# Where the output norms of a kernel's tail put their rows: a ring of five buffers, or eleven tiles that are no longer used

## The chip, the cores and the metric

The kernel runs on one core of a Trainium2 chip. The metric is the device time of one execution in microseconds, as the median of several runs. Engines are named as in the profile: PE is TensorE's matmul row, PEld its weight loads, DVE is VectorE, ACT is ScalarE, POOL is GpSimd and SP is the engine that issues most of the DMAs.

## What is computed

The reference is one conformer block on x of shape 2 x 4000 x 144 in bf16, with four heads of 36:

```python
h = _layernorm(x);  x = x + 0.5 * (_silu(h @ w_ff1a) @ w_ff1b)
h = _layernorm(x);  q, k, v = heads(h @ w_qkv)
p = _softmax(q @ k.T * Dh ** -0.5);  x = x + merge(p @ v) @ w_o
h = _layernorm(x);  a, b = split(h @ w_pw1);  h = a * _sigmoid(b)
c = sum(shift(h, i - 2) * dw[i] for i in range(5))
x = x + _silu(c) @ w_pw2
h = _layernorm(x);  x = x + 0.5 * (_silu(h @ w_ff2a) @ w_ff2b)
return _layernorm(x)
```

This change is about the last line: the layernorm that makes the output, and its way out to memory.

## The kernel before

The 8000 tokens are cut into 16 chunks of 500 (NCH = 16), each held as four blocks of 125 rows in the tile X. Attention over all keys takes most of the time: for each chunk of queries, scores go to PSUM, their exponentials are written by ACT or DVE to one of eleven tiles of PT (128 x 1000 bf16, 2000 bytes a partition), and PE multiplies them with the values. The other stages of the chunks (first feed-forward, projections, gated unit and convolution, second feed-forward, norms) are threaded between the attention's pieces, and what is left of them after the last attention product is the tail.

The program is first recorded: each call of `op` notes an instruction, what it reads and writes by key, and from the history of these keys the earlier instructions that it must wait for. Then `settle` (line 2140) and `arrange` (465) put the instructions of each engine into an order that is written out in a table (ORDER). `finish` (535) turns the dependencies into semaphore waits and drops those that another wait of the same engine already covers, and `replay` (579) emits them. So each engine works through a fixed queue, and an instruction that waits holds up all behind it on its engine. Almost every instruction has line 589 in the profile, because `replay` issues them there; they are told apart by their tiles.

A layernorm is `ln` (1236). It takes one of five buffers u of XN (NXN = 5, line 795; 2048 bytes a partition each), makes statistics on DVE (tile ST, key MV), the scale on POOL or DVE with POOL's power (tile RS, keys VE and RS), and then one instruction for each block of 125 rows on DVE, POOL or ACT that writes the normed rows to XN[u] (key XN). Two kinds of user come next:

- Norms ahead of a matmul (`ln_tr`, 1308): the rows are transposed, by PE through PSUM for small parts of the last chunks and by a DMA on SP for whole chunks.
- Output norms (`store`, 1872, with `store=True`): the rows lie packed in XN[u] (the view XNC, 1020) and `put` (1866) issues one DMA that writes them to the output. In the tail this DMA may be issued by SP or by ACT.

The buffer's key orders its users: the next norm with the same u writes after the last transposes or the last store have finished reading. A store has finished when its DMA has landed, so a norm can wait for a store. The statistics' keys order the same way, but only norms read them.

In the tail (`mode["tail"]`, set at 2450, after the last attention product is recorded) nine output norms are recorded: chunk 9, chunk 10, chunk 14's blocks 2 and 3, its blocks 0 and 1, chunk 13, chunk 11, chunk 12, and chunk 15's two halves. Chunks 14 and 15 go in halves of two blocks. On DVE's queue stand, in this order: chunk 9's output norm, chunk 15's second-half norm ahead of its gated unit, chunk 10's output norm, the output norm of chunk 14's blocks 0 and 1, the norm of chunk 12 ahead of its second feed-forward (four instructions), the norms of chunk 15's second and first half ahead of theirs (two each), and then the output norms of chunks 13, 12 and of chunk 15's first half. Chunk 11's output norm is POOL's; those of chunk 14's and 15's second halves are ACT's.

PSUM has eight banks. The last two (BX = 6 and 7) hold the attention sums; once the attention is over, bank 6 is given to the other stages as well (2452).

Of the kernel before, what the change touches and what calls it, by code (L numbers as in the profile page):

```python
# [12 lines left out]
D = 144  # L13
H = 4
DH = 36
HD = 72
# [5 lines left out]
TB = 125  # L22
NB = 4
CH = 500
# [269 lines left out]
    'ddadppdadppdddddppdpddppdppdddddddddddppadadppdddppadppddddddppdddddppdadappdppddppddddppdppdddppddp'  # L294
    'pdddppddpddppddappdddppdppddddppddpddppddppddppddddddpppdddaapppdddaadppdppppddddapddddaaddddddaaddd'
    'addddpdddpddadddddddpdpddpddapddddddpddaaddddad'
)
ALPHABET = '!#$%&()*+,-./0123456789:;<=>?@ABCDEFGHIJKLMNOPQRSTUVWXYZ[]^_`abcdefghijklmnopqrstuvwxyz{|}~'

# [5 lines left out]
def c_dve(n, rate=1.0):  # L305
    return n / (960 * rate) + 0.07
# [456 lines left out]
def bass_standalone__conformer_family_zipformer__speech_kernel(  # L763
# [24 lines left out]
    R = Rec(nc)  # L788
# [178 lines left out]
    XN = sb("XN", [NXN, NB, 2, 128])  # L967
# [14 lines left out]
    PT = sb("PT", [NPT, 2, CH])  # L982
# [31 lines left out]
    BX = 6  # L1014
    PTU = PT[:, :, :, :].rearrange("p a b n -> p (a b n)").bitcast(U16).rearrange("p (a b n) -> p a b n", a=NPT, b=2)
# [4 lines left out]
    XNC = XN[:, :, :, :, :].rearrange("p u i k n -> p u (i k n)")[:, :, 0:NB * D].rearrange("p u (i d) -> p u i d", i=NB)  # L1020
# [126 lines left out]
        Slots(R, range(n)) for n in (NXN, NXT, NTH - 2, NHT, NSW, NAN, NPT))  # L1147
    thw = Slots(R, [NTH - 2])
    wide = Wide(banks)
    mode = {"front": True, "tail": False}  # L1150
    silus = [6]

    def small(c):
# [81 lines left out]

    def ln(c, bs, e=False, store=False):
        n, b0, rows = len(bs), bs[0], TB + e
        xn = (lambda u, j: XNC[0:rows, u, j, :]) if store else (lambda u, j: XN[0:rows, u, j, :, 0:HD])
        xi = (lambda j: X[0:rows, c * NB + b0 + j, :]) if store else (lambda j: halves(X[0:rows, c * NB + b0 + j, :]))
        xe = ["XE"] * e  # L1240
        u = yield need("dve", xnp)
        for j in range(0, n, 2):
            op("dve", "bn_stats", ST[0:rows, u, j:j + 2, :].rearrange("p i k -> p (i k)"),
               xv(c, range(b0 + j, b0 + j + 2), rows).rearrange("p i d -> p d i"),
               r=[("X", c, b0 + j), ("X", c, b0 + j + 1)] + xe, w=[("MV", u)], cost=0.365)
        calm = small(c)
        if n == NB and not calm and not store and ("XN", u) not in clear:
            clear.add(("XN", u))
            yield need("pool")
            op("pool", "memset", XN[:, u, :, :, :], 0.0, w=[("XN", u)], cost=0.8)  # L1250
        yield need("dve" if calm else "pool", hold=calm)
        a = (RS[0:rows, u, 1, 0:n], ST[0:rows, u, 0:n, 2], 1.0 / D, LN_EPS)
        k = dict(op0=ALU.mult, op1=ALU.add)
        o = op("dve" if calm else "pool", "tensor_scalar", *a, **k, r=[("MV", u)], w=[("VE", u)], cost=0.08 if calm else 0.28)
        if calm:
            R.unit([o], "d", {"p": [("pool", "tensor_scalar", a, k, 0.28, None)]})
            yield need("pool")
        else:
            R.unit([o], "p", {"d": [("dve", "tensor_scalar", a, k, 0.08, None)]})
            R.step += 1  # L1260
        op("pool", "tensor_tensor", RS[0:rows, u, 0, 0:n], RS[0:rows, u, 1, 0:n], NHALF[0:rows, 0:n], op=ALU.pow,
           r=[("VE", u), "NHALF"], w=[("RS", u)], cost=0.7 if calm else POW_COST)
        NM = RS[0:rows, u, 2, 0:n]
        signs = {"p": ("pool", "tensor_scalar", (NM, ST[0:rows, u, 0:n, 1], -1.0, None), dict(op0=ALU.mult), 0.24, None, None, ()),
                 "a": ("dve", "scalar_tensor_tensor", (), dict(
                     out=NM, in0=ST[0:rows, u, 0:n, 1], scalar=-1.0, in1=RS[0:rows, u, 0, 0:n], op0=ALU.mult, op1=ALU.mult),
                     0.08, None, None, ())}
        if not calm:
            code = "p"
            R.step += 1  # L1270
        elif mode["tail"] and R.free["act"] + XSLACK < R.free["dve"]:
            code = "a"
            yield need("dve", hold=True)
        else:
            code = "d"
            yield need("dve")
        pre = []
        if code in signs:
            g = signs.pop(code)
            pre = [op(g[0], g[1], *g[2], **g[3], r=[("MV", u)] + [("RS", u)] * (code == "a"), w=[("NM", u)], cost=g[4])]  # L1280
            if code == "a":
                yield need("act")
            R.step += 1
        alts, ops = {"d": [], "p": [], "a": []}, []
        for j in range(n):
            sc = RS[0:rows, u, 0, j:j + 1]
            k = dict(op1=ALU.mult)
            alts["d"].append(("dve", "tensor_scalar", (xn(u, j), xi(j), ST[0:rows, u, j, 1:2], sc), dict(
                op0=ALU.subtract, op1=ALU.mult), 0.231, None))
            alts["p"].append(("pool", "tensor_scalar", (xn(u, j), xi(j), RS[0:rows, u, 2, j:j + 1], sc), dict(  # L1290
                op0=ALU.add, op1=ALU.mult), XN_COST, XN_LAT))
            alts["a"].append(("act", "activation", (xn(u, j), xi(j), ACT.Identity),
                              dict(bias=RS[0:rows, u, 2, j:j + 1], scale=sc), 0.41, None))
            eng, name, a, k, cost, lat = alts[code][-1]
            ops.append(op(eng, name, *a, **k, r=[("X", c, b0 + j), ("MV", u), ("RS", u)] + [("NM", u)] * bool(pre) + xe,
                          w=[("XN", u)], cost=cost, lat=lat))
        alts.pop(code)
        deps = [(d, True) for key in (("MV", u), ("RS", u)) for d in R.history(key)[0]]
        R.unit(ops, code, alts, {q: [g[:7] + (deps,)] for q, g in signs.items()}, pre=pre)
        R.step += 1  # L1300
        return u

    XSLACK = 3.2
    XN_COST = 0.5
    XN_LAT = 0.4
# [534 lines left out]
    def post2(c):  # L1840
        cc = c % CPB
        last = cc == CPB - 1
        z = yield need("pe", swp, cond=lambda: c in glu_done and (last or c == NCH - 2 or c + 1 in glu_done))
        e = c == NCH - 1
# [21 lines left out]
        def put(dst, src, u):  # L1866
            q = f"o{len(outs)}"
            act = mode["tail"] and R.free["act"] < R.free["sp"]
            op("act" if act else "sp", "dma_start", dst, src, q=q, r=[("XN", u)], cost=0.4 if act else 0.7)
            outs.append(q)  # L1870

        def store(bs):
            n, b0, b1 = len(bs), bs[0], bs[-1] + 1
            u = yield from ln(c, bs, e and 3 in bs, True)
            if c == NCH - 2 and 3 in bs:
                put(out_tok[c][0:TB - 1, b0:b1, :], XNC[0:TB - 1, u, 0:n, :], u)
                if n > 2:
                    put(out_tok[c][TB - 1:TB, b0:2, :], XNC[TB - 1:TB, u, 0:2, :], u)
            else:
                put(out_tok[c][:, b0:b1, :], XNC[0:TB, u, 0:n, :], u)  # L1880
            if e and 3 in bs:
                put(out_tok[c - 1][TB - 1:TB, 2:4, :], XNC[TB:TB + 1, u, 0:2, :], u)
            xnp.give(u)

        def part(bs):
# [10 lines left out]
        ps = parts(c)  # L1896
# [103 lines left out]
            return (PTI[:, z, :, :], PSV[:, lo:hi + 1:hi - lo, 0:CH], EXP_BIAS, 0.0), k  # L2000
        return (PTI[:, z, hh, :], PSV[:, lo, 0:CH], EXP_BIAS, 0.0), k

    def ymw_args(what, z, y):
        zu, yu = (PTU[:, q, :, :].rearrange("p b n -> p (b n)") for q in (z, y))
        zf, yf = (PT[:, q, :, :].rearrange("p b n -> p (b n)") for q in (z, y))
        bits = dict(op0=ALU.bitwise_and, op1=ALU.bitwise_or)
        if what == "y":
            return "tensor_scalar", (yu, zu, 0x7F, 0x3F00), bits
        if what == "m":
            return "tensor_tensor", (yf, zf, yf), dict(op=ALU.mult)  # L2010
        return "tensor_scalar", (zu, zu, 0x7F80, 2), bits
# [122 lines left out]
    for c in range(CPB):  # L2134
        S.add(pre(c), R.ready(("X", c, 0), "dve"), rank=-1 if c == 0 else 1)

    COST = dict(S=0.2105, E=c_act(2 * CH), R=c_act(CH), z=c_dve(CH), x=c_dve(2 * CH), y=c_dve(2 * CH, 4),
                m=c_dve(2 * CH, 2), w=c_dve(2 * CH, 4))

    def settle():  # L2140
        R.choose(UNITS)
# [23 lines left out]
        for k, ops in old.items():  # L2165
            if k[1] == "O":
                sum_deps.setdefault(R.phase[k[0]], {}).update({id(d): (d, raw) for d, raw in outside(ops) if not raw})
        where = 0
        for n in range(NIT):
            ph, c, t = its[n]  # L2170
            rest = t == NF
# [24 lines left out]
            else:  # L2196
# [7 lines left out]
                else:  # L2204
# [5 lines left out]
                deps, last = [(z, True) for z in zs], None  # L2210
                chain = {}
                for i, what in enumerate("ymw"):
                    name, a, k = ymw_args(what, *sl)
                    more = [] if last is None else [(last, True if what == "m" else False)]
                    chain[what] = last = fresh("dve", name, a, k, COST[what], "e", deps + more, (n, what), 2 + i)
                chain["w"].deps.append((chain["y"], False))
                made = {0: (zs, [chain["w"]]), 1: ([chain["y"]], [chain["m"]])}
# [281 lines left out]
```

## Time and profile before

| | |
|---|---|
| median of 3 runs | 868.47 us (868.26 to 868.83) |
| span of the profiled execution, first to last instruction | 866.2 us |
| the execution's time beyond its span, taken as the median less the span | 2.3 us |
| granted TensorE clock over the span | 0.999 |
| last attention product on PE | 820.8 us |
| last instruction of DVE on data | 861.9 us |
| PE busy | 849.7 us (98%) |
| DVE busy | 835.1 us (96%) |
| ACT busy | 834.9 us (96%) |

No other time of the profiled execution is given than its span, so the execution's own time is put at the median. All times in the traces are microseconds from the start of the span. In a row of the timeline stand the start, the length, the engine, the line, the operation, the tile written and those read, the shape, and the number of instructions that were merged into the row; in brackets is the idle time of the engine just before the row and what ended it. A row such as `XN<-X,ST,RS` is a norm, `out_dram<-XN` a store of normed rows, `X<-PS,X` a residual addition out of PSUM, and `PS<-IDENT,XN` a transpose on PE.

### The profile page before, as it was taken

How to read it: one execution, taken by the hardware profiler on the slowest of the kernel's cores; microseconds unless marked ns; L12 is line 12 of the kernel's file. 1: busy time of each engine (PE TensorE's matmuls, PEld its weight loads, DVE VectorE, ACT ScalarE, POOL GpSimd, SP SyncE). 2: the span in 40 equal slices, each digit the busy share in tenths (PEclk: the TensorE clock that was granted, in tenths of full speed). 3: DMA queues.
4: the chain of work that ended last, by engine and by line, in shares of the span. 5: the costliest groups of instructions: out<-in, count | busy, mean ns of one | idle time of the engine just before them, and what ended most of it. 6: DMA issues, size and time to landing. Idle time of an engine off the chain costs nothing.

```text
span 866.2 us, 27018 instructions
## 1 busy us (share of the span) xinstructions
PE 849.7 (98%) x11585; PEld 412.0 (48%) x11585; DVE 835.1 (96%) x1819; ACT 834.9 (96%) x1096; POOL 283.2 (33%) x562
## 2 busy tenths in 40 slices
PE   9999999999999999999999999999999999999996
PEld 8644434444344444444444444445444444445585
DVE  7999999999999999999999999999999999999986
ACT  6999999999999999999999999999999999999975
POOL 7771331041334301441230060320550173300854
PEclk9999999999999999999999999999999999999999
DMA  3331111102113110211210020110130021100121
GB/s 102 83 54 21 33 21 38 21 14 45 34 26 51 17 24 2 51 27 39 33 39 2 2 44 3 21 26 14 26 49 4 12 48 39 26 2 14 41 47 50
DMA packets 86331, 26.92 MB, mean 31 GB/s; under 512 B 81384, under 2 KB 86210, under 8 KB 86210
## 3 DMA queue, kind: packets, MB, share of 16 engines
q1 hardware_dynamic: 84662, 24.34, 15.0%
q8 instruction: 91, 1.49, 0.7%
q10 hardware_dynamic: 1548, 0.84, 0.4%
q14 instruction: 30, 0.25, 0.1%
HBM read 3.31 MB, written 2.30 MB: 6 GB/s over the span
## 4 chain that ended last, share of the span: by engine, by line
ACT 40%; PE 40%; DVE 17%; DMA 1%; issue 0%; POOL 0%; DVEq 0%; ACTq 0%
PE PS L589 40%; ACT PT L589 37%; DVE PT L589 12%; ACT TH L589 3%; DVE ST L589 1%; DVE QT L589 1%; DVE HT L589 1%; DVE U L589 1%; DVE X L589 1%; DMA X<-in_x_dram 0%; DMA out_dram<-XN 0%; DVE XN L589 0%; DVE KT L589 0%; ACT X L589 0%; DVE AN L589 0%
## 5 line engine op out<-in xcount | busy, mean ns | idle before, releaser
L589 ACT ACTIVATE PT<-PS 128x1000 bf16<-128x1000 f32 (+1 forms) x793 | 730.0, 1072 | 4.9 <-PE PS L589 4.1
L589 PE MATMUL PS<-QT,KT 64*64 64x500 bf16 x3968 | 460.2, 383 | 4.2 <-ACT PT L589 1.2
L589 PE MATMUL PS<-PT,VA 64*37 64x500 bf16 x4828 | 449.6, 372 | 1.3 <-DVE QT L589 0.5
L589 DVE TENSOR_SCALAR PT<-PS 128x500 int16<-128x500 f32 x425 | 279.8, 678 | 4.3 <-PE PS L589 2.9
L589 PEld LDWEIGHTS PS<-QT,KT 64*64 64x64 bf16 x3968 | 139.8, 104 | 201.9 <-ACT PT L589 99.9
L589 PEld LDWEIGHTS PS<-PT,VA 64*37 64x37 bf16 x4828 | 163.1, 96 | 105.5 <-issue 16.2
L589 POOL TENSOR_SCALAR RS<-ST 125x4 f32<-125x4 f32 (+1 forms) x132 | 31.0, 237 | 479.9 <-DVE ST L589 476.0
L589 DVE TENSOR_SCALAR PT<-PT 128x1000 uint16<-128x1000 uint16 x430 | 172.6, 419 | 1.8 <-DVE PT L589 0.2
L589 DVE TENSOR_TENSOR PT<-PT 128x1000 bf16<-128x1000 bf16 x215 | 144.9, 678 | 0.8
L589 POOL TENSOR_SCALAR XN<-X,RS 125x144 bf16<-125x144 bf16 x250 | 142.4, 581 | 3.9 <-POOL RS L589 0.5
L589 POOL TENSOR_TENSOR RS<-RS,NHALF 125x4 f32<-125x4 f32 (+2 forms) x93 | 92.0, 993 | 50.7 <-DVE RS L589 48.6
L589 ACT ACTIVATE TH<-PS 128x500 bf16<-128x500 f32 (+3 forms) x175 | 92.8, 560 | 3.5 <-PE PS L589 3.0
L589 DVE SCALAR_TENSOR_TENSOR HT<-TH,PS 128x500 bf16<-128x500 bf16 (+1 forms) x120 | 71.5, 616 | 0.8 <-ACT TH L589 0.5
L589 PE MATMUL PS<-XTB,WA 72*128 72x500 bf16 (+2 forms) x280 | 71.3, 359 | 0.6 <-DVE PT L589 0.2
L589 DVE BATCH_NORM_STATS2 ST<-X 125x6 f32<-125x288 bf16 (+1 forms) x160 | 65.6, 449 | 1.9 <-DMA X<-in_x_dram 1.2
L589 DVE SCALAR_TENSOR_TENSOR X<-PS,X 125x288 bf16<-125x288 f32 x114 | 50.8, 451 | 6.7 <-PE PS L589 5.6
L589 PE MATMUL PS<-WB,HT 128*125 128x144 bf16 (+1 forms) x640 | 52.2, 229 | 0.1
L589 PEld LDWEIGHTS PS<-WB,HT 128*125 128x125 bf16 (+1 forms) x640 | 44.9, 136 | 13.4 <-issue 3.9
L589 PEld LDWEIGHTS PS<-XTB,WA 72*128 72x128 bf16 x280 | 21.5, 97 | 28.9 <-issue 8.3
L589 PE MATMUL PS<-U,DG 128*128 128x375 bf16 (+7 forms) x204 | 28.0, 263 | 0.1
L589 POOL COPY U<-U 128x2 bf16<-128x2 bf16 (+1 forms) x54 | 10.6, 229 | 42.5 <-DVE U L589 32.3
L589 ACT ACTIVATE HT<-PS 128x500 bf16<-128x500 f32 (+3 forms) x43 | 20.6, 537 | 3.4 <-PE PS L589 2.9
(95 smaller groups left out, 522.1 us busy)
## 6 DMA issues: line engine op xcount, KB each, us to landing
X<-in_x_dram SPq DMA_DIRECT2D x16, 140.6 KB
XTQ<-XTB SPq DMA_DIRECT2D x24, 70.3 KB
out_dram<-XN SPq DMA_DIRECT2D x12, 140.6 KB
XTB<-XN SPq DMA_TRANSPOSE x53, 3.6
out_dram<-XN ACTq DMA_DIRECT2D x2, 140.6 KB
XTB<-AN SPq DMA_TRANSPOSE x15, 3.2
WA<-in_w_ff1a_dram ACTq DMA_DIRECT2D x1, 144.0 KB
WB<-in_w_ff1b_dram ACTq DMA_DIRECT2D x1, 144.0 KB, 2.6
```

The lines of the kernel that those rows point to most:

```text
L589: ins = getattr(eng, o.name)(*o.a, **o.k)
```

## The change

An output norm that is recorded in the tail no longer writes to the buffer XN[u]. The first of them writes to tile 0 of PT, the next to tile 1, and so on to tile 8 for the ninth; each tile is used once. Its store reads from there. The norm keeps its number u for its statistics and scales. Three things follow for the waits:

- The norm's instructions drop what they would have waited for because of XN[u].
- In their place they wait for the instructions that last wrote banks 6 and 7 of PSUM as the program is recorded. For bank 7 these are the last attention sums, after which no probability is read. Bank 6 has by then been used by other stages, so the wait is for a matmul of theirs.
- A norm of another kind that gets the same u later drops the tail norms and their stores from what it waits for.

The core of the diff:

```diff
     def ln(c, bs, e=False, store=False):
         n, b0, rows = len(bs), bs[0], TB + e
-        xn = (lambda u, j: XNC[0:rows, u, j, :]) if store else (lambda u, j: XN[0:rows, u, j, :, 0:HD])
+        late = store and mode["tail"]
+        if late:
+            at.append(XPT[:, len(at)])
+            row = at[-1]
+        xn = (lambda u, j: (row[0:rows, j, :] if late else XNC[0:rows, u, j, :])) if store else (lambda u, j: XN[0:rows, u, j, :, 0:HD])
...
         u = yield need("dve", xnp)
+        if late:
+            out_of[u] = row
...
+            h = R.history(("XN", u))
+            before = {id(o) for o in h[0] + h[1]}
             ops.append(op(eng, name, *a, **k, r=[("X", c, b0 + j), ("MV", u), ("RS", u)] + [("NM", u)] * bool(pre) + xe,
                           w=[("XN", u)], cost=cost, lat=lat))
+            if late:
+                spare.add(id(ops[-1]))
+                for o in R.hist["ps", BX][0] + R.hist["ps", BX + 1][0]:
+                    ops[-1].deps.append((o, False))
+            ops[-1].deps = [d for d in ops[-1].deps if id(d[0]) not in (before if late else spare)]
...
+    at, out_of, spare = [], {}, set()
+    XPT = PT[:, :, :, :].rearrange("p a b n -> p a (b n)")[:, :, 0:NB * D].rearrange("p a (i d) -> p a i d", i=NB)
...
             op("act" if act else "sp", "dma_start", dst, src, q=q, r=[("XN", u)], cost=0.4 if act else 0.7)
             outs.append(q)
+            if mode["late"]:
+                spare.add(id(R.ops[-1]))
...
             u = yield from ln(c, bs, e and 3 in bs, True)
+            mode["late"] = u in out_of
+            rows = out_of.pop(u, XNC[:, u])
...
-                put(out_tok[c][:, b0:b1, :], XNC[0:TB, u, 0:n, :], u)
+                put(out_tok[c][:, b0:b1, :], rows[0:TB, 0:n, :], u)
```

The rest of the diff prepares `settle` to let two attention tiles of DVE share their instructions, by a table PAIRS. The table is empty here, so each tile gets the same instructions with the same dependencies as before. The orders (ORDER) and all other tables are as they were.

More of the change, by code (lines that the diff above doesn't have):

```diff
@@ L296 @@
     'addddpdddpddadddddddpdpddpddapddddddpddaaddddad'
+)
+PAIRS = (
 )
@@ L1149, in bass_standalone__conformer_family_zipformer__speech_kernel @@
     wide = Wide(banks)
-    mode = {"front": True, "tail": False}
+    mode = {"front": True, "tail": False, "late": False}
     silus = [6]
@@ L1874, in store @@
             u = yield from ln(c, bs, e and 3 in bs, True)
+            mode["late"] = u in out_of
+            rows = out_of.pop(u, XNC[:, u])
             if c == NCH - 2 and 3 in bs:
-                put(out_tok[c][0:TB - 1, b0:b1, :], XNC[0:TB - 1, u, 0:n, :], u)
+                put(out_tok[c][0:TB - 1, b0:b1, :], rows[0:TB - 1, 0:n, :], u)
                 if n > 2:
-                    put(out_tok[c][TB - 1:TB, b0:2, :], XNC[TB - 1:TB, u, 0:2, :], u)
+                    put(out_tok[c][TB - 1:TB, b0:2, :], rows[TB - 1:TB, 0:2, :], u)
             else:
-                put(out_tok[c][:, b0:b1, :], XNC[0:TB, u, 0:n, :], u)
+                put(out_tok[c][:, b0:b1, :], rows[0:TB, 0:n, :], u)
             if e and 3 in bs:
-                put(out_tok[c - 1][TB - 1:TB, 2:4, :], XNC[TB:TB + 1, u, 0:2, :], u)
+                put(out_tok[c - 1][TB - 1:TB, 2:4, :], rows[TB:TB + 1, 0:2, :], u)
             xnp.give(u)
@@ L2001, in z_args, with ymw_args, view @@
         return (PTI[:, z, hh, :], PSV[:, lo, 0:CH], EXP_BIAS, 0.0), k
-    def ymw_args(what, z, y):
-        zu, yu = (PTU[:, q, :, :].rearrange("p b n -> p (b n)") for q in (z, y))
-        zf, yf = (PT[:, q, :, :].rearrange("p b n -> p (b n)") for q in (z, y))
+    def ymw_args(what, z, y, z2=None, y2=None):
+        def view(t, q, q2):
+            if q2 is None:
+                return t[:, q, :, :].rearrange("p b n -> p (b n)")
+            lo, hi = min(q, q2), max(q, q2)
+            return t[:, lo:hi + 1:hi - lo, :, :].rearrange("p q b n -> p q (b n)")
+        assert z2 is None or (z < z2) == (y < y2)
+        zu, yu, zf, yf = (view(t, *q) for t in (PTU, PT) for q in ((z, z2), (y, y2)))
         bits = dict(op0=ALU.bitwise_and, op1=ALU.bitwise_or)
@@ L2137, in bass_standalone__conformer_family_zipformer__speech_kernel @@
     COST = dict(S=0.2105, E=c_act(2 * CH), R=c_act(CH), z=c_dve(CH), x=c_dve(2 * CH), y=c_dve(2 * CH, 4),
-                m=c_dve(2 * CH, 2), w=c_dve(2 * CH, 4))
+                m=c_dve(2 * CH, 2), w=c_dve(2 * CH, 4), y2=c_dve(4 * CH, 4), m2=c_dve(4 * CH, 2), w2=c_dve(4 * CH, 4))
     def settle():
@@ L2167, in settle @@
                 sum_deps.setdefault(R.phase[k[0]], {}).update({id(d): (d, raw) for d, raw in outside(ops) if not raw})
-        where = 0
+        parts, lead = [], dict(PAIRS)
+        led = set(lead.values())
         for n in range(NIT):
@@ L2209, in settle @@
                         readers[n, hh, bk[hh]] = zs
[L2210 to L2217, printed above, removed]
+                made = zs
+            parts.append((n, ph, rest, kind, sl, made))
+        chains = {}
+        for n, ph, rest, kind, sl, zs in parts:
+            if kind not in "DW" or n in led:
+                continue
+            m = lead.get(n)
+            wide = () if m is None else tuple(parts[m][4])
+            zs = zs if m is None else zs + parts[m][5]
+            deps, last = [(z, True) for z in zs], None
+            chain = {}
+            for i, what in enumerate("ymw"):
+                name, a, k = ymw_args(what, *sl, *wide)
+                more = [] if last is None else [(last, True if what == "m" else False)]
+                chain[what] = last = fresh("dve", name, a, k, COST[what + "2" if wide else what], "e", deps + more,
+                                           (n, what), 2 + i)
+            chain["w"].deps.append((chain["y"], False))
+            chains[n] = chain
+            if m is not None:
+                chains[m] = chain
+        for n, ph, rest, kind, sl, made in parts:
+            if kind in "DW":
+                chain = chains[n]
+                made = {0: (made, [chain["w"]]), 1: ([chain["y"]], [chain["m"]])}
             v_deps = [(d, raw) for d, raw in outside(old[n, "O"]) if raw]
```

## Prediction, made before the changed kernel was run

> **What bounds the kernel now.** Only output norms recorded after the last attention product change, so I read the tail. The first view is the busy time of each engine in stretches; columns are the stretch, its length, then PE, PEld, DVE, ACT and POOL.
>
> ```profile
> 830.00:840.00 10.00, 10.00 (x116) 8.51 (x115) 9.23 (x33) 7.99 (x18) 6.97 (x11) 1.00 0.33 64
> 840.00:850.00 10.00, 9.39 (x101) 6.95 (x98) 8.66 (x30) 7.14 (x17) 4.84 (x9) 1.00 0.14 37
> ```
>
> TensorE is full from 830 to 840; between 840 and 850 it lacks 0.61 us. So anything gained in the tail must come out of that hole, or from what follows the last matmul. The second view is the chain that ended last (start, length, what).
>
> ```profile
> 844.52 3.92 DMA out_dram<-XN
> ...
> 848.53 0.67 DVE XN L589 x3
> ...
> 850.00 0.04 issue
> 850.04 8.19 PE PS L589 x92
> ```
>
> A store of an output norm, issued at 844.52, lands at 848.44 and only then six DVE norms run; TensorE waits for them until 850.04 and is alone on the chain for the next 8.19 us. The third view gives both engines there, with the idle time before a row in brackets.
>
> ```profile
> 847.12 0.46 DVE L589 BATCH_NORM_STATS2 ST<-X 125x6 f32<-125x288 bf16 x1
> 848.53 1.45 DVE L589 TENSOR_SCALAR XN<-X,ST,RS 125x144 bf16<-125x144 bf16 x6 [0.95 <-DMA out_dram<-XN]
> 849.90 0.82 DVE L589 SCALAR_TENSOR_TENSOR X<-PS,X 125x288 bf16<-125x288 f32 x2
> 848.49 0.75 PEld L589 LDWEIGHTS PS<-WB,HT 128*125 128x125 bf16 x10
> 850.04 0.25 PEld L589 LDWEIGHTS PS<-IDENT,XN 126*72 126x72 bf16 x4 [0.80 <-DVE XN L589]
> 848.60 0.79 PE L589 MATMUL PS<-WB,HT 128*125 128x144 bf16 x10
> 850.04 0.41 PE L589 MATMUL PS<-IDENT,XN 126*72 126x126 bf16 x4 [0.65 <-DVE XN L589]
> 850.29 1.42 PE L589 MATMUL PS<-WB,HT 128*125 128x144 bf16 x20
> ```
>
> DVE is free at 847.58 and stands for 0.95 us; the weight loader stands for 0.80 us, the matmul row (whose ends are modelled) for 0.65.
>
> **The change, part by part.** Read off the code: nine output norms are recorded in the tail, those of chunks 9 to 13 and both halves of 14 and 15. Each gets its own tile of PT, so it no longer waits for what used its XN buffer, and a later norm in that XN buffer no longer waits for the store. All the rest stays: engines, orders, instruction counts, shapes, store issues.
>
> *Waits removed.* In the tail four DVE norms wait for a store: the second norm of chunk 15 ahead of its gated unit (on chunk 9's store), the output norm of chunk 14's first half (on its second half's store), the norm of chunk 12 ahead of its feed-forward (on chunk 10's store, the one in the chain), and the norm of chunk 15's second half behind it (on chunk 14's other store). Only two cost idle time:
>
> ```profile
> DVE XN L589 <- DMA out_dram<-XN: 1.5, 2, 0.9
> 838.33 0.54 DVE L589 TENSOR_SCALAR XN<-X,ST,RS 125x144 bf16<-125x144 bf16 x2 [0.57 <-DMA out_dram<-XN]
> 838.86 0.97 DVE L589 SCALAR_TENSOR_TENSOR X<-PS,X 125x288 bf16<-125x288 f32 x2
> 841.98 0.82 DVE L589 SCALAR_TENSOR_TENSOR X<-PS,X 125x288 bf16<-125x288 f32 x2
> 837.92 1.41 PE L589 MATMUL PS<-WB,HT 128*125 128x144 bf16 x20
> 839.17 0.39 PE L589 MATMUL PS<-IDENT,XN 125*72 125x125 bf16 x4
> ```
>
> *The wait at 838.33* is worth nothing. DVE would start 0.54 us earlier, but the two residual additions behind it read sums that TensorE makes from 837.92 on, 20 matmuls at 1.25/20 = 0.0625 us each (837.92 to 839.17). The last one's own time is 1.41 - 19 x 0.0625 = 0.22. The first addition needs the tenth, out at 837.92 + 9 x 0.0625 + 0.22 = 838.70, so it could start some 0.1 us sooner; the second needs the twentieth, whose modelled end is 839.33. The pair takes 0.97 us here against 0.82 where nothing holds it (841.98): the second already waits for TensorE, and from there on DVE is where it was. TensorE itself goes from the 20 matmuls to the transposes at 839.17 without a hole. Bounds: 0 to 0.54; I take 0. It can't be below nothing, since no order changes.
>
> *The wait at 848.53* is the term. Without it the first of the six starts when DVE is free and its scale is there. POOL makes the scales:
>
> ```profile
> 845.63 1.01 POOL L589 TENSOR_TENSOR RS<-RS,NHALF 125x4 f32<-125x4 f32 x1
> 847.10 0.69 POOL L589 TENSOR_TENSOR RS<-RS,NHALF 126x2 f32<-126x2 f32 x1
> 848.04 0.70 POOL L589 TENSOR_TENSOR RS<-RS,NHALF 125x2 f32<-125x2 f32 x1
> 847.74 1.44 ACT L589 ACTIVATE HT<-PS 128x500 bf16<-128x500 f32 x3 [0.26 <-PE PS L589]
> 845.73 0.26 SPq L589 DMA_DIRECT2D out_dram<-XN  x1
> 849.56 1.23 SPq L589 DMA_TRANSPOSE XTB<-XN  x1
> ```
>
> Chunk 12's is ready at 846.64, chunk 15's at 847.79. So the six run from about 847.60: 848.53 - 847.60 = 0.93 us sooner, ending at 850.00 - 0.93 = 849.07. The fifth and sixth no longer wait for the store issued at 845.73; if they did, at the 3.92 us of the other store, it would land at 849.65 and give back most of the gain. The old trace shows it landed before the fifth norm at 849.50 and no closer.
>
> *What is late next on TensorE.* Its ten matmuls from 848.60 end their issue at 848.60 + 10 x 0.0625 = 849.23, and the loader is free at 848.49 + 0.75 = 849.24. The norms, at 849.07 plus the 0.04 of issue seen before 850.04, are there 0.13 us ahead. So the transposes start at 849.24 instead of 850.04: 0.80 by the loader. The matmul row would be free at 849.23, 0.81 sooner; its first matmul can trail its load by 0.1 (848.49 and 848.60), which leaves 0.70. Of 0.70 to 0.81 I take **0.78**, by the loader, whose times aren't modelled.
>
> *Does the rest move as one?* The next matmuls (850.29, then 849.51) take weights that ACT finishes at 847.74 + 1.44 = 849.18: 0.33 to spare. The second of the two residual additions (849.90) needs those ten matmuls, modelled end 848.60 + 0.79 = 849.39; moved, it would start near 849.4, so it loses a few hundredths. Its followers on DVE are not on the chain; the norms behind them (850.63) would end near 850.3 and TensorE wants them near 850.76. SP's transpose of chunk 12 (849.56) moves up 0.9 with its norms, and SP's queue is empty since the store at 845.73. From 850.04 the 8.19 us are TensorE alone; after them everything is released by it.
>
> *Waits added.* Each tail norm also waits for the last attention sums and for whatever last wrote bank 6. For eight of the nine its engine has already waited for a later matmul. The ninth, chunk 11's on POOL, gains one:
>
> ```profile
> 853.06 1.86 PE L589 MATMUL PS<-XTB,WA 72*128 72x500 bf16 x8
> 855.04 1.79 POOL L589 TENSOR_SCALAR XN<-X,RS 125x144 bf16<-125x144 bf16 x4
> 856.86 3.79 SPq L589 DMA_DIRECT2D out_dram<-XN  x3
> 860.39 1.86 ACTq L589 DMA_DIRECT2D out_dram<-XN  x3
> ```
>
> Its matmul is the last of the eight, out at 853.06 + 1.86 = 854.92, and the norm starts at 855.04; both move together. It costs 0 to 0.1 us for POOL, behind which stand only POOL's later scales (next at 858.12 by the same view) and on SP the first of three stores at 856.86; the last stores are ACT's. I take 0.
>
> *Writing into PT* is not shown for these norms. Bounds: nothing, since DVE already writes PT's eleven tiles with a narrow spread, and the dearest norm of this stretch.
>
> ```profile
> L589 DVE TENSOR_SCALAR PT<-PT x25: 400/415/483, 782.2 to 819.3; 128x1000 uint16<-128x1000 uint16 x25
> L589 DVE TENSOR_SCALAR XN<-X,ST,RS x24: 300/312/427, 843.4 to 861.6; 125x144 bf16<-125x144 bf16 x22, 126x144 bf16<-126x144 bf16 x2
> ```
>
> Only the last two of DVE's norms would count on the path: 2 x (0.427 - 0.312) = 0.23 at most; I take 0, as the first row is nearest.
>
> *DVE beside POOL.* The six norms move from a stretch where POOL stands to one where it makes powers (847.10 to 848.74).
>
> ```profile
> 843.42 0.98 DVE L589 TENSOR_SCALAR XN<-X,ST,RS 125x144 bf16<-125x144 bf16 x4
> 843.87 0.69 POOL L589 TENSOR_TENSOR RS<-RS,NHALF 125x2 f32<-125x2 f32 x1
> 856.45 1.10 DVE L589 TENSOR_SCALAR XN<-X,ST,RS 125x144 bf16<-125x144 bf16 x4
> ```
>
> Four norms beside a power take 0.98 (0.245 each), six alone 1.45 (0.242 each), four beside POOL's norms 1.10. So 0.02 for the six, and at most 0.12 x 6/4 = 0.18, of which 0.13 is covered. I take 0.
>
> **Sum.** The profiled execution spans 866.2 us; 868.47 - 866.2 = 2.27 lies around it and is carried over. 866.2 - 0.78 = 865.4; on the median 868.47 - 0.78 = **867.7**.
>
> **Rivals.**
>
> *POOL's powers take the place of the wait.* If DVE stood still while POOL makes powers, the six would lose 847.60 to 847.79 and 848.04 to 848.74, 0.89 us, end at 849.96, and TensorE would start at 850.0: the gain is gone, 868.4. For it: the margin is only 0.13, so even 0.3 lost to POOL costs 0.17. Against: the norms at 843.42 ran at full speed beside a power. The Trainium skill (Advanced Engine Details and Errata, VectorE Performance Modes) speaks for it, in that VectorE's two-port modes and GpSimd share a port and block each other; the trace disagrees for a power (0.245 against 0.242) and agrees for POOL's norms (1.10 against 0.98).
>
> *The change doesn't do what it says.* A wait on a store stays, since a norm or its statistics still depend on the XN buffer's old users: 868.5. Against: statistics and scales are read by norms, never by stores.
>
> *The stores at the end read slower.* A PT tile is 2000 bytes a partition, an XN buffer 2048, so store rows start at other offsets; stores are what the end waits for.
>
> ```profile
> q10 hardware_dynamic: 260, 0.22, 14.3%
> 863.00:864.00 1.00, 0.00 (x0) 0.00 (x0) 0.00 (x0) 0.00 (x0) 0.00 (x0) 0.84 0.32 106
> q1 hardware_dynamic: 1996, 0.61, 63.5%
> ```
>
> The first two are of the end (862 to 867 with packets, MB and share, and one us of it, whose second last figure is the DMA share): ACT's queue took 14.3% of 16 engines for 5 us, 11.4 engine-us; the peak share of 0.32 is about 5 engines, so 2.29 us each. The last (835 to 840, transposes beside a store) has the dearest bytes of the tail: 63.5% x 80 / 0.61 = 83 us per MB against 11.4 / 0.22 = 52, a factor of 1.6. With it 2.29 x 0.6 = 1.37 comes back: 867.7 + 1.37 = **869.1**, slower than before. It decides from 0.78 / 2.29, that is from packets 1.34 times as long. Nothing in the trace shows that the start matters. The Trainium skill (DMA: Bandwidth & Descriptors, How a descriptor splits into AXI transactions) says that it does: a read begins at the 256-byte boundary below its start and pays for the unused bytes, 25 beats in place of 18 for 576 bytes at worst; an estimate by it is up to 1.39 on such rows and 1.2 on those of 1152, some 0.5 us, so 868.2.
>
> **Chances.** Forecast 0.72 (its own range 867.3 to 868.1); POOL in DVE's way 0.08 (up to 868.4); norms not freed 0.05 (868.5); slower stores 0.15 (any factor up to 1.6, so up to 869.1). The range goes down to both idle times in full, 868.47 - 0.95 - 0.57 = 866.95, rounded to 867.0, and up to 868.8, a factor of 1.48 on the stores, which leaves out their dear end. A difference under 0.2% (1.7 us) is about what a measurement of this kernel can't tell from no change. Faster by more needs over both idle times together: 0.03. Slower by more needs store packets over twice as long: 0.03. Within: 0.94.
>
> **What would show it.** Right: no DVE idle time put down to a store in the tail, the hole of 0.65 before chunk 15's transposes gone, those at about 849.3, the last matmul near 858.1 instead of 858.9, the span 865.4. The wait at 838.33 gone too, with the transposes at 839.17 unmoved. Wrong: a hole of like size with another releaser; or an unchanged end after an earlier last matmul, with a larger DMA share of ACT's queue, which would be the stores.

## The result

The changed kernel takes 867.07 us (median of 21 runs, 866.27 to 867.84) against 868.32 for the kernel before (21 runs beside them, 867.66 to 869.26): a ratio of 0.9986, with a 95% interval of 0.9980 to 0.9993. So it is 1.25 us faster, between 0.6 and 1.7 us. The forecast was 0.78 us, inside that interval; the trace shows which part of the rest the forecast had not seen.

### The profile page after: what moved, and what is told of

It is laid out like the page before. It is cut to its first block, busy times and chain, and to the rows that moved or that the text cites. A ratio compares the mean times of both kernels' runs of the same rounds, so it can differ in the third digit from the quotient of the medians.

```text
span 865.7 us, 27015 instructions
## 1 busy us (share of the span) xinstructions
PE 849.3 (98%) x11585; PEld 411.3 (48%) x11585; DVE 835.4 (96%) x1819; ACT 835.0 (96%) x1096; POOL 284.8 (33%) x562
## 4 chain that ended last, share of the span: by engine, by line
ACT 40%; PE 40%; DVE 16%; DMA 1%; POOL 1%; issue 0%; ACTq 0%; SPq 0%; DVEq 0%; POOLq 0%
PE PS L591 40%; ACT PT L591 37%; DVE PT L591 11%; ACT TH L591 3%; DVE ST L591 1%; DVE QT L591 1%; DVE X L591 1%; POOL XN L591 1%; DVE HT L591 1%; DVE U L591 1%; DMA XTB<-XN 1%; DMA X<-in_x_dram 0%; DMA WE<-in_w_ff1a_dram 0%; DVE KT L591 0%; ACT X L591 0%
```

## The profile after

The first view is again the busy time of each engine in stretches (length, then PE, PEld, DVE, ACT and POOL), here of the changed kernel.

```profile
830.00:840.00 10.00, 10.00 (x118) 8.54 (x116) 9.36 (x34) 8.62 (x20) 7.85 (x16) 1.00 0.21 44
840.00:850.00 10.00, 10.00 (x114) 7.71 (x112) 9.52 (x32) 7.33 (x18) 4.94 (x10) 1.00 0.25 57
```

TensorE's 9.39 us between 840 and 850 have become 10.00: the hole is gone. The chain that ended last says the same (start, length, what).

```profile
835.95 22.30 PE PS L591 x249
858.25 0.02 issue
858.27 0.42 ACT X L591
...
861.74 0.23 DVE PT L591
```

No store stands on it any more; one stretch of TensorE's work runs from 835.95 to the last matmul. The timeline shows how the two waits ended (idle time before a row and its releaser in brackets).

```profile
837.73 1.44 DVE L591 TENSOR_SCALAR XN<-X,ST,RS 125x144 bf16<-125x144 bf16 x6
839.69 0.46 DVE L591 SCALAR_TENSOR_TENSOR X<-PS,X 125x288 bf16<-125x288 f32 x1 [0.45 <-PE PS L591]
847.99 0.46 DVE L591 BATCH_NORM_STATS2 ST<-X 125x6 f32<-125x288 bf16 x1
848.36 1.44 DVE L591 TENSOR_SCALAR XN<-X,ST,RS 125x144 bf16<-125x144 bf16 x6
849.46 0.79 PE L591 MATMUL PS<-WB,HT 128*125 128x144 bf16 x10
850.09 0.38 PE L591 MATMUL PS<-IDENT,XN 126*72 126x126 bf16 x4
847.96 0.74 POOL L591 TENSOR_TENSOR RS<-RS,NHALF 126x2 f32<-126x2 f32 x1
848.91 0.77 POOL L591 TENSOR_TENSOR RS<-RS,NHALF 125x2 f32<-125x2 f32 x1
```

The whole tail stands 0.86 us later here (the ten matmuls at 849.46, not 848.60), because the attention ahead of it differs by that much between the two executions, though DVE, ACT, POOL and SP do the same instructions there in the same order. So times must be read from a point inside the tail. From the ten matmuls to the transposes it is now 850.09 - 849.46 = 0.63 us, and was 850.04 - 848.60 = 1.44: **0.81 us**, the hole. The six norms follow their statistics at once. The wait ahead of the six norms at 837.73 is gone too, and DVE now stands 0.45 us for TensorE at 839.69: that time was given back, as forecast. POOL's two powers run beside the moved norms and take 0.74 and 0.77 us; the norms take 1.44.

The end is the second part. Here is DVE's last row in the kernel before,

```profile
860.48 1.46 DVE L589 TENSOR_SCALAR XN<-X,ST,RS 125x144 bf16<-125x144 bf16 x6
```

and in the changed kernel:

```profile
860.50 1.46 DVE L591 TENSOR_SCALAR PT<-X,ST,RS 125x144 bf16<-125x144 bf16 x6
```

They end at 861.94 and 861.96, but the spans end at 866.25 and 865.70: 4.31 us behind in the one and 3.74 in the other, **0.57 us** that no step of the forecast has. 0.81 + 0.57 = 1.38. The DMA view of 862 to 867 shows where they are: a strip of 40 slices of 0.125 us with the busy tenths of 16 DMA engines, what they moved, and the packets, MB and share of each queue. Before:

```profile
DMA  0012121522323333333111000000000000000000
GB/s 9 0 55 46 46 74 65 130 65 101 111 92 138 115 101 124 106 111 106 60 46 37 23 18 18 5 0 0 0 0 0 0 0 0 0 0 0 0 0 0
...
q14 instruction: 1, 0.01, 0.4%
```

After:

```profile
DMA  0013324223332333333221000000000000000060
GB/s 14 0 55 55 83 74 111 46 65 92 120 92 92 115 120 111 106 111 111 69 65 37 0 0 0 0 0 0 0 0 0 0 0 0 0 0 0 0 131 0
...
q10 hardware_dynamic: 260, 0.22, 14.9%
```

Both work at 2 to 3 tenths, about five engines of 16. Before, the last four busy slices move only 23, 18, 18 and 5 GB/s: one engine is still at its part while the other four are done. After, the last slice still has 37, then nothing. Before there is also one packet of 8 KB in queue 14, which carries instructions and not data; after there is none in queue 14. The packets of the stores themselves take a like share (14.9% against 14.3%).

## Experiments

The theory after this reading had two parts: the wait on chunk 10's store made the hole (0.8 us), and something else, tied to the one wait added on POOL (chunk 11's norm, on bank 6), shortens the end (0.5 us). Medians of such kernels are good to some 0.8 us, so each profile is also measured inside its tail, between four points: the start a of the row of 21 matmuls `PS<-U,DG` (843.53 before, 844.39 after), the start b of the transposes `PS<-IDENT,XN 126*72`, the end c of DVE's last norm and the end d of the span. c - b is 11.87 to 11.91 in all of them. All times are us; the last but one column compares d - a with 22.72 before; fetch is the packet of queue 14 nearest to the end.

| kernel | b - a | d - c | fetch | d - a, change | ratio, 95% interval |
|---|---|---|---|---|---|
| before | 6.51 | 4.31 | 862.89 | | |
| after | 5.70 | 3.74 | 856.32 | -1.41 | 0.9986 (0.9980 to 0.9993) |
| e1_place_only | 6.56 | 3.75 | 856.54 | -0.50 | 0.9997 (0.9988 to 1.0007) |
| e2_in_keys | 5.69 | 3.72 | 855.80 | -1.43 | 0.9988 (0.9980 to 0.9997) |
| e3_chunk10_only | 6.28 | 3.94 | 862.57 | -0.59 | 0.9998 (0.9989 to 1.0007) |
| e4_chunk9_only | 6.68 | 4.13 | 862.40 | -0.01 | 1.0000 (0.9992 to 1.0009) |
| e5_three_norms | 5.69 | 4.16 | 862.25 | -0.98 | 0.9988 (0.9980 to 0.9997) |
| e6_no_bank6 | 5.69 | 4.31 | 862.09 | -0.83 | 0.9989 (0.9980 to 0.9998) |
| e7_wait_only | 6.53 | 3.75 | 856.52 | -0.53 | 0.9995 (0.9986 to 1.0004) |
| e8_split_ends | 5.70 | 2.67 | 856.49 | -2.48 | 0.9977 (0.9967 to 0.9986) |
| e9_second_norm | 6.55 | 3.97 | 862.32 | -0.29 | 0.9996 (0.9987 to 1.0004) |
| e10_double_wait | 6.52 | 3.69 | 846.85 | -0.61 | 0.9995 (0.9986 to 1.0003) |
| e11_cut10 | 5.69 | 4.27 | 861.48 | -0.88 | 0.9999 (0.9990 to 1.0007) |
| e12_cut_no_pt | 6.03 | 3.27 | 862.12 | -1.55 | 0.9984 (0.9975 to 0.9993) |

### The place without the waits' removal, and another place

e1 writes the rows into PT but keeps every old wait:

```diff
-            ops[-1].deps = [d for d in ops[-1].deps if id(d[0]) not in (before if late else spare)]
```

> The nine output norms write to PT as in the changed kernel, but keep every wait on the XN buffer's old users. The theory (all of the gain is the hole before chunk 15's transposes): no gain, a ratio to before of 1.000 within 0.0006, with DVE's idle time of about 0.95 us put down to a store and TensorE's hole of about 0.65 us still there. The rival (the place of the rows makes the stores at the end land sooner, since the span ends 3.7 us after DVE's last norm in the changed kernel's profile and 4.3 us in that of before): about 0.5 us faster, ratio 0.9994, and an end of about 3.7 us.

It took 867.85 us, beside 868.21 for the kernel before. Two views of it, the waits and the timeline:

```profile
DVE XN L591 <- DMA out_dram<-PT: 1.5, 2, 1.0
```

```profile
850.31 0.41 PE L591 MATMUL PS<-IDENT,XN 126*72 126x126 bf16 x4 [0.70 <-DVE XN L591]
```

The stores now come from PT, DVE waits for them as before, and the hole stays. So the place alone doesn't close it. But the end is the changed kernel's (3.75), as the rival of this run had it. That doesn't yet show that the place shortens it, since e1 also keeps the wait added on bank 6; e6 and e7 below part the two.

e2 keeps the removal of the waits and puts the rows into the tile of the keys, dead by then as well, at 2048 bytes from tile to tile in place of 2000:

```diff
-    XPT = PT[:, :, :, :].rearrange("p a b n -> p a (b n)")[:, :, 0:NB * D].rearrange("p a (i d) -> p a i d", i=NB)
+    XPT = KT[:, :, :, :].rearrange("p a b n -> p (a b n)")[:, 0:9 * 1024].rearrange("p (a n) -> p a n", a=9)[:, :, 0:NB * D].rearrange("p a (i d) -> p a i d", i=NB)
```

> All waits as in the changed kernel, but the nine norms write into the tile of the keys, which is as dead by then, at 2048 bytes a row instead of 2000. The theory: as the changed kernel, 0.8 us faster than before (ratio 0.9991), no hole on TensorE between 840 and 850 us, and an end after DVE's last norm that differs from 3.7 us by chance only. The rival: the hole is gone as well, but the end is back at 4.3 us if PT's place or pitch made it short.

It took 867.10 us, beside 868.21, with no hole and an end of 3.72. Which of these two dead tiles takes the rows makes no difference that the times or the trace show.

### Which norms the hole needs

e3, e4 and e5 give only some norms a tile of PT (`c == 9` in e4, `c in (10, 14)` in e5):

```diff
-        late = store and mode["tail"]
+        late = store and mode["tail"] and c == 10
```

> Only chunk 10's output norm writes to PT: the wait in the chain goes, the one of chunk 15's second-half norm on chunk 14's store stays. In the trace of before that store landed at 849.16 us. The theory: it is late next; the last two of the six norms start at about 849.2 instead of 848.6 us (on that trace's clock) and TensorE's hole shrinks from 0.65 to about 0.3 us, so the gain is 0.3 us (ratio 0.9996). The rival (only the wait in the chain matters): the whole 0.8 us.

> Only chunk 9's output norm writes to PT, so only the wait at 838.33 us goes. The theory: no gain (ratio 1.000 within 0.0006); DVE's idle time of 0.57 us goes there, the residual additions behind it still wait for TensorE, and the hole of 0.65 us before chunk 15's transposes stays. The rival (both waits count): 0.3 to 0.5 us faster, ratio 0.9995.

> Only the output norms of chunk 10 and of both halves of chunk 14 write to PT, so the wait in the chain and the one behind it go and the one at 838.33 us stays. The theory: the whole gain, 0.8 us (ratio 0.9991), the hole of TensorE gone, DVE's idle time of about 0.57 us for a store still there. The rival: 0.3 to 0.5 us short of the changed kernel's 1.25 us because chunk 9's wait is left.

e4 took 868.33 us, beside 868.21 for the kernel before; the hole stays, and only chunk 9's wait is gone: worth nothing, as forecast. e5 took 867.19, with no hole and with chunk 9's wait still there, so the three norms of chunks 10 and 14 hold all of the hole's gain. e3 took 868.09 (beside 868.33). Its DVE in the timeline:

```profile
847.91 0.98 DVE L591 TENSOR_SCALAR XN<-X,ST,RS 125x144 bf16<-125x144 bf16 x4
849.62 0.55 DVE L591 TENSOR_SCALAR XN<-X,ST,RS 126x144 bf16<-126x144 bf16 x2 [0.74 <-DMA out_dram<-XN]
```

Four norms run at once, and the last two wait for chunk 14's store instead. The hole shrinks to 0.43 us, where about 0.3 was expected. Two waits stood one behind the other, and with the first away the second shows. The forecast had put it like this: if the fifth and sixth still waited, their store would take back most of the gain.

### What shortens the end

e6 is the changed kernel without the wait on bank 6; e7 is the kernel before with that wait on chunk 11's norm and nothing else.

```diff
-                for o in R.hist["ps", BX][0] + R.hist["ps", BX + 1][0]:
+                for o in R.hist["ps", BX + 1][0]:
```

```diff
+            if store and mode["tail"] and c == 11:
+                for o in R.hist["ps", BX][0]:
+                    ops[-1].deps.append((o, False))
```

> The changed kernel without the wait for bank 6: the tail's norms wait for the last attention sums alone, so POOL's queue loses the one wait that the change had added there. New theory (two parts: 0.8 us from TensorE's hole, and about 0.45 us because the added instruction on POOL's queue moves an 8 KB fetch of instructions from 862 us, where it shares a DMA engine with the last stores, to 856 us): the fetch on queue 14 is back near 862 us, the span ends about 4.2 us after DVE's last norm instead of 3.7, and the gain falls to 0.8 us (ratio 0.9991). The rival (the place of the rows sets the end): still 3.7 us, ratio 0.9986 to 0.9988.

> The kernel before, with only the wait for bank 6 added ahead of chunk 11's output norm on POOL, and no norm moved to PT. New theory: the fetch on queue 14 moves from 862 to 856 us, the end after DVE's last norm falls from 4.3 to about 3.7 us, TensorE's hole stays; 0.45 us faster (ratio 0.9995). The rival (place): end of 4.1 to 4.3 us and no gain.

e6 took 867.38 and e7 867.76 us, both beside 868.33. e6 has no hole and the long end (4.31), e7 has the hole and the short end (3.75). So the two parts of the gain are separate: in the tail lengths -0.83 and -0.53 add up to -1.36, beside -1.41 for both at once. The DMA view of e6 from 862 to 867 has the instruction packet again:

```profile
q10 hardware_dynamic: 231, 0.18, 11.9%
q14 instruction: 1, 0.01, 0.4%
```

Does this wait act by what it orders, or by being one instruction more? The first norm of chunk 11 already waits for POOL's own sum, so a second wait there needs an instruction of its own; the norm behind it waits for nothing. e9 hangs the same wait on that second norm (`and j == 1` behind `c == 11` in e7's edit), where it costs no instruction. e10 instead writes a wait twice that is long met, that of chunk 14's power:

```diff
                         eng.wait_ge(self.sems[lane], v)
+                        if e == "pool" and o is mine[-18]:
+                            eng.wait_ge(self.sems[lane], v)
```

> The kernel before, with the bank-6 wait hung on chunk 11's second norm on POOL instead of its first. The first norm already waits for POOL's own sum, so a wait there is an instruction of its own; the second norm waits for nothing else, so the wait rides on it and POOL's instruction count stays as before. Theory (one more POOL instruction shifts the 8 KB instruction fetch away from the last stores): nothing shifts; the fetch lies beside the last stores at about 862.5, the span ends 4.1 to 4.3 us after DVE's last norm, time as before, 868.3. Rival (the wait itself, by delaying that norm or by what it orders, shortens the end): end at 3.7 to 3.8 us, about 867.8, as in the run with the wait on the first norm.

> The kernel before, with one wait on POOL (that of chunk 14's power, long satisfied by the first copy) written twice: one more POOL instruction that orders nothing new. Theory (instruction fetch): as with the bank-6 wait, the 8 KB fetch moves to about 856, no fetch from 862 on, the span ends 3.7 to 3.8 us after DVE's last norm, about 867.8; the hole of 0.6 to 0.8 us ahead of chunk 9's transposes stays. Rival (it is what the bank-6 wait orders): end at 4.1 to 4.3 us, 868.3.

e9 took 867.65 and e10 867.32 us, beside 868.12; these medians don't part them, and e9's lies nearer to its rival's 867.8 than to the 868.3 expected. The profiles do part them. e9, with the wait but no instruction more, has the packet and ends 3.97 us behind DVE, between the 4.1 expected and the rival's 3.8 (DMA view, 862 to 867):

```profile
q10 hardware_dynamic: 260, 0.22, 14.0%
q14 instruction: 1, 0.01, 0.9%
```

e10, with one instruction more that orders nothing, has no packet there and ends 3.69 behind; the hole, which is ahead of chunk 15's transposes, stays (0.66 us):

```profile
DMA  2332332333333333221000000000000000000000
...
q10 hardware_dynamic: 260, 0.22, 14.5%
```

So in these runs it is the instruction's presence. e10's packet did not go to 856 as expected; it stands at 846.85. In the table, the five kernels whose last stores are whole and have no packet of queue 14 beside them end 3.69 to 3.75 us behind DVE, the seven that have one 3.94 to 4.31. The semaphore events of the last store, in which each of its five engines reports its end, say the same: beside a packet the fifth engine is 0.20 to 0.60 us behind the fourth, without one at most 0.10.

### The stores themselves

A store of 125 rows works on five DMA engines. e8 is the changed kernel with its last two stores cut into rows 0 to 111 and 112 to 124, each part issued on ACT:

```diff
-                put(out_tok[c][:, b0:b1, :], rows[0:TB, 0:n, :], u)
+                cut = 112 if mode["late"] and (c == 12 or e and b0 == 0) else TB
+                put(out_tok[c][0:cut, b0:b1, :], rows[0:cut, 0:n, :], u)
+                if cut < TB:
+                    free, mode["cut"] = (dict(R.free), R.issue, R.last), True
+                    put(out_tok[c][cut:TB, b0:b1, :], rows[cut:TB, 0:n, :], u)
+                    (R.free, R.issue, R.last), mode["cut"] = free, False
```

> The changed kernel with the last two stores (chunk 12 and chunk 15's first half) each cut into rows 0 to 111 and 112 to 124, both pieces on ACT's queue. If a store of 125 rows runs on 5 of the 16 DMA engines (its share of 0.31 to 0.32) and one of 112 rows on 16, the packets of the last two stores, 2.29 us on each of 5 engines, take about 0.7 us on 16, and the end after DVE's last norm falls from 3.7 to about 2.8 us in spite of two more issues of 0.3 us on ACT: 2.1 us faster than before (ratio 0.9976). If the stores run on 16 engines anyhow, nothing or 0.3 us slower than the changed kernel.

866.12 us, beside 868.33: the fastest kernel here. Its DMA view, 862 to 867:

```profile
DMA  0037896303951100000000000000000000000000
GB/s 5 0 83 221 212 304 203 120 9 106 249 143 37 42 0 0 0 0 0 0 0 0 0 0 0 0 0 0 0 0 0 0 0 0 0 0 0 0 0 0
```

Two short bursts on up to 9 tenths of the engines take the place of a long stretch on 3, and the end falls from 3.74 to 2.67 us. The Trainium skill (DMA: Bandwidth & Descriptors, Why a DMA increments its semaphore by 16 and not by 1) says that a transfer is spread over the largest number of engines up to 16 that divides its rows; by that, 125 rows go to 5, 112 to 16, 13 to 13, and the trace agrees: five engines report for the whole store, 16 and 13 report for the parts of the cut ones.

e11 asks whether chunk 10's store had to be late at all: the kernel before, with that one store cut in the same way (the condition is `mode["tail"] and c == 10`) and no tile of PT. e12 cuts this one and the last two (`c in (10, 12) or e and b0 == 0`).

> The kernel before, with chunk 10's store alone cut into rows 0 to 111 and 112 to 124, both issued on ACT. Theory (the hole was a store on 5 DMA engines of which one was late behind an instruction fetch): the store lands about 1.7 us after its issue, near 846.5, DVE is not free for its slot's next norm before 847.6, so the wait vanishes and with it the hole, without any move to the probability tiles: about 867.5; the extra issue on ACT (0.3 us) may take back up to 0.3. Rival (the landing comes late however the store is cut): the hole stays at 0.6 to 0.8 us, 868.3.

> The kernel before with the ring of five rows, and chunk 10's store and the last two stores cut into rows 0 to 111 and 112 to 124. If the two cuts do all that the change and the cut of its last stores do together: 866.1 to 866.5, end 2.6 to 2.8 us after DVE's last norm, no hole. If the move to the probability tiles is needed for the hole: 867.0 to 867.3, with the hole still there.

The timeline of e11, DVE and PE:

```profile
847.04 0.46 DVE L589 BATCH_NORM_STATS2 ST<-X 125x6 f32<-125x288 bf16 x1
847.50 1.45 DVE L589 TENSOR_SCALAR XN<-X,ST,RS 125x144 bf16<-125x144 bf16 x6
849.15 0.39 PE L589 MATMUL PS<-IDENT,XN 126*72 126x126 bf16 x4
```

The six norms still have their wait on the store, and it no longer costs anything: no idle time, no hole. The store's last part has landed at 847.38, only 0.12 us ahead of the norms and not near 846.5 as expected: a packet of queue 14 stands at 846.00, and most parts had landed by 846.65. So either way closes the hole. e11's median is 868.09 us beside 868.12, where its tail length says 0.88 less; the interval reaches from -0.9 to +0.6 us, so whether the profile's gain is in the median stays open. e12 took 866.44 us, 1.7 less than before, with no tile of PT at all. Its end is 3.27 us, where 2.6 to 2.8 was expected and e8 has 2.67. ACT's last four issues say why, in e12 and then in e8:

```profile
861.23 2.20 ACTq L589 DMA_DIRECT2D out_dram<-XN  x4
```

```profile
861.48 1.62 ACTq L591 DMA_DIRECT2D out_dram<-PT  x4
```

The third of them takes 0.94 us in e12 and 0.36 in e8. From the end of the last issue to the last landing it is 1.01 and 0.98 us, so it was the issue that came late, not the parts. A packet of queue 14 stands beside that issue (862.12); whether it held the issue up isn't shown. The hole is gone in e12 too, yet b - a is 6.03 rather than 5.70. ACT's rows in its timeline show why:

```profile
845.13 0.90 ACTq L589 DMA_DIRECT2D out_dram<-XN  x1
845.15 0.27 ACT L589 ACTIVATE SW<-PS 80x126 bf16<-80x126 f32 x1
846.08 0.38 ACT L589 ACTIVATE SW<-PS 128x250 bf16<-128x250 f32 x1 [0.65 <-PE PS L589]
```

The second part's issue holds ACT's queue for 0.90 us (0.41 in e11), and the next eviction starts only behind it, at 846.08 (the row names PE as its releaser, but e11's same eviction stood 0.16). TensorE waits for that eviction: its next product starts 0.72 us behind the two matmuls ahead of it (845.79 to 846.51), 0.43 in e11.

## Why the prediction was right, and where it was short

The forecast, 867.7 with a gain of 0.78, lies in the measured interval, and its main step held, with one link missing. The measured 867.07 is below the forecast's own range (867.3 to 868.1) and just inside the lower end of the full one, 867.0. That end was set by both idle times in full. The one at 838.33 turned out to be worth nothing, and 0.57 us at the end of the kernel came in its place, so it is by luck that the full range reached down far enough.

- *The wait at 848.53.* Forecast 0.70 to 0.81, taken 0.78; the trace has 0.81, and e5 and e6, which still have the packet beside the last stores, have 0.82 in b - a. In e3, where the wait on chunk 10's store alone is removed, four norms went at once.
- *Why that store was late* is the missing link. In the kernel before, four of the five engines report the end of chunk 10's store at 847.03 to 847.38 and the fifth at 848.43. Without this one engine the hole would not have been: DVE was free at 847.58. A packet of queue 14 stands at 847.05 in that trace. Chunk 10's store is whole in twelve of the kernels. In the seven with a packet there (846.75 to 847.32), its fifth engine is 0.67 to 1.26 us behind the fourth; in the five without, at most 0.11. In those five, the changed kernel among them, the packet stands at 842.78 to 843.65, beside the store of chunk 14's blocks 2 and 3. Now that store has an engine 0.69 to 1.22 us late (845.90 against 844.88 in the changed kernel), and nothing waits for it. Chunk 10's store is done at 848.24 there, ahead of the six norms' start at 848.36. So the changed kernel no longer needed the wait's removal to close the hole. In e3 the packet stays at 847.29, and there it was the removal that let the four norms go. No run removes all the waits with the packet still there, so how much of the 0.81 us the removal would give by itself isn't measured.
- *The wait at 838.33* is worth nothing: DVE waits for TensorE behind it, and e4 shows no gain.
- *Writing into PT, DVE beside POOL*: the last six norms take 1.46 us into PT as into XN. The six behind the hole take 1.44 us beside two powers, against 1.45 with POOL idle for all but the first 0.21 us. The rival in which POOL takes the wait's place fails. POOL's powers lost the little there was, 0.05 and 0.07 us.
- *The stores at the end read slower*: 14.9% against 14.3% of the engines' time is 1.04 times, where 1.34 was needed to undo the gain. The Trainium skill (DMA: Bandwidth & Descriptors, How a descriptor splits into AXI transactions) would have a read that starts at a 256-byte boundary cheaper. The trace shows no such price: with no packet beside the stores, the ends are 3.74 and 3.75 us from PT (after, e1), whose tiles lie 2000 bytes apart, and 3.72 and 3.75 from the keys' tile and from XN (e2, e7), where they lie 2048 apart. At which offset from a boundary each tile starts isn't in the trace.
- *The change frees the norms*: it does, no wait on a store is left.

The step that was short is the one sentence "All the rest stays: engines, orders, instruction counts, shapes, store issues", and with it the 0 taken for the added wait. The first lines of the page of the kernel before and of the changed one:

```profile
span 866.2 us, 27018 instructions
```

```profile
span 865.7 us, 27015 instructions
```

Four waits left DVE's stream (1898 instructions in the trace before, 1894 after, with those that only wait) and one came into POOL's (582 and 583). That one was costed by the time for which it holds POOL's norm, and it holds it for nothing that counts. Its effect came by another way, as e7, e9 and e10 show: one instruction more, another time of an instruction fetch, an end without a late engine, 0.57 us. Nothing in the forecast's views could give its size, but the packet in queue 14 and the four slow slices stood in the old trace; the forecast read that view for the share of queue 10 alone.

Open is how the fetch's time follows from the count: the added wait moved it by 6 us, e10's by 16. For which engine's instructions a packet of queue 14 comes isn't in the trace, so that DVE's fewer waits moved the one at 847.05 is argued from e3 and e4 (one wait less, not moved) and e5 and e6 (three and four less, moved to 843.35 and 842.78), and not shown by itself. Also open is why a packet that lasts 0.31 us in its record makes an engine of a store late by 0.54 or 1.05, as in the kernel before. That the packet and the late part share a DMA engine is the likely reading; no record names the engine of either.

## What to carry to other kernels

When a norm or another writer waits for a store, look at the store first: here it was on five engines with one of them late, and cutting its rows so that they spread over 16 closed the same hole in the trace as a buffer of its own. The last stores of a kernel are worth the same look, as nothing hides them: 1.07 us here, nearly as much as the whole change. And below some 0.2%, compare lengths inside the traces as well as medians, and count the instructions: one wait more or less can move an instruction fetch onto or off a transfer that the end waits for.

## What the runs showed of the hardware

- Instruction fetches get in the way of data transfers. The Trainium skill (Runtime: NRT & Kernel Launch, Instruction fetch mechanics) says that a fetch is mostly hidden, and that blocks are of 16 KiB. Here blocks of 16 KB stand in queue 8 and of 8 KB in queue 14 (30 packets, 0.25 MB), so those of queue 14 are half as large. Whether they are hidden for the engines that execute, no run here shows; for stores they aren't: a packet of queue 14 beside a store came with one of its engines late, in the kernel before by 1.05 us for chunk 10's and 0.54 for the last, and the late engine moved with the packet from kernel to kernel.
- An extra DMA issue on ACT isn't free even in a queue with idle time: 0.41 us in e11 and 0.90 in e12 for the same small store, the latter with TensorE waiting behind it. Why it takes longer at one time than at another is open.
